# A register load tied behind a transposing transfer, and one k load traced five steps earlier, in an attention and expert kernel

## The chip, the cores and the metric

The kernel runs on one core of a Trainium2 chip. The metric is the device time of one execution in microseconds (us). Times below are either such a time or positions and durations in one execution that the hardware profiler recorded.

The engines are named as in the profile: PE (TensorE, with PEld for its weight loads), DVE (VectorE), ACT (ScalarE), POOL (GpSimd) and SP (SyncE), which here issues nearly all transfers. Each engine works through its own row of instructions in order, and an instruction that has to wait holds up all that stand behind it.

## The reference

Three blocks follow each other. The first is attention with random features for 4 batches of 8 heads, 576 tokens and 64 channels. `phi` projects q and k to 128 features and takes an exponential; each head then needs only `kv` and `z`, sums over the tokens.

```
q_p, k_p = (phi(q_s), phi(k_s))
kv = np.einsum('bhsm,bhsd->bhmd', k_p, v)
z = np.sum(k_p, axis=2)
num = np.einsum('bhsm,bhmd->bhsd', q_p, kv)
den = np.einsum('bhsm,bhm->bhs', q_p, z)[..., None] + 1e-06
return num / den
```

Its output, 2304 tokens of 512 channels, goes to a layer of 8 experts, in which every token belongs to the expert with the largest logit.

```
expert_idx = np.argmax(x @ w_gate, axis=1)
for e in range(E):
    xe = x[expert_idx == e]
    out[expert_idx == e] = gate_w * (np.maximum(xe @ w1[e], 0.0) @ w2[e])
```

The third block is a plain feed-forward layer, `h = x @ w_in`, `g = h / (1 + exp(-1.702 h))`, `g @ w_out`, with 2048 hidden channels.

## The kernel before

**Attention in quarters.** Each batch's 8 heads go in two halves of 4 heads, so there are 8 such pieces (the code's index `i`, called quarters here; `QB` is 2, the number of pieces of one batch). For each piece `kgen` makes the features of k and the sums `kv`, and `qgen` the features of q, the quotient (`num`, N in the code, L444) and its transposition for the experts (`tx`, `small`, L464 to L473). Ahead of that a piece has to be loaded and turned: `load_qk` (L253, L258) loads it to `m`, and `halves_T` splits it into two half-precision parts `hl` (ACT makes the first, POOL or DVE the second, L307 and L308), turns them with a transposing transfer on SP, `xT<-hl` (L309), and asks for the sums of squares. The projection `pr` (L350, L351) reads `xT`. `qgen` is a list of steps such as P0, X0, N0, each of which yields. In step number `KPRE` = 6 of piece `i` it loads k's piece `i + 2` and calls `halves_T` for it.

**Routing and experts.** After the second piece of a batch, `route_steps` computes the logits, counts the tokens of each expert (`ct_ps`, L561) and takes the expert with the most, `es` (L571). The expert's number comes into a register of SP by `values_load` (L604, a TENSOR_LOAD), and by that register `stage` loads the weights of that expert in 8 chunks of 512 KB, the first in two parts, from `w1` and `w2` (L674, `st<-in_moe_w_dram`). `rr` holds each token's expert and gate, and is stored by L609 and L612. `split_w` splits each chunk into a rounded part `wh` (ACT, L698) and the rest `wl` (POOL, the first chunk DVE, L700), and an expert matmul consists of three products of such parts (`mm3`, L136, `m_ps`).

**What sets the order.** The code is traced in one thread in which attention and experts take turns. A scheduler then places every instruction in the row of its engine by a simulated timeline of its own, so code that is traced in another place can move instructions on all engines. Loads, stores and transposing transfers share SP's row. A transfer is issued when the row comes to it and its inputs are there. Under `tc.high_priority()` stand the weight loads of the first batch. `tc.add_manual_dep` with the class NoSync says to the scheduler that one instruction comes after another on the same engine; no semaphore is waited on for it.

Of the kernel before, what the change touches and what calls it, by code (L numbers as in the profile page):

```python
# [22 lines left out]
def kernel(  # L23
# [13 lines left out]
    nc = tc.nc  # L37
# [24 lines left out]
    XQ = nc.sync  # L62
    DVE_LO = 1
    KPRE = 6
# [117 lines left out]
    NJ = 9  # L182
    QB = H // QH
    NQ = B * QB
    asked = []
    clock = [0]
    late = []

# [77 lines left out]
    def square_sum(m, c, sq, folds):  # L266
        nc.gpsimd.tensor_tensor(out=m[:, c], in0=m[:, c], in1=m[:, c], op=ALU.mult)
        w = D
        for _ in range(folds):
            w //= 2  # L270
            o = sq[:, c].unsqueeze(2) if w == 1 else m[:, c, 0:w]
            nc.gpsimd.tensor_tensor(out=o, in0=m[:, c, 0:w], in1=m[:, c, w:2 * w], op=ALU.add)
        if w > 1:
            nc.vector.tensor_reduce(out=sq[:, c], in_=m[:, c, 0:w], axis=AX.X, op=ALU.add)
        nc.scalar.activation(out=sq[:, c], in_=sq[:, c], func=ACTF.Copy, scale=sq_scale)

    def turned(src, i):
        m = src[i]
        xT = att.tile([P, NJ, P], F32, tag="xT", name="xT", bufs=3)
        sq = att.tile([P, NB], F32, tag="sq", name="sq", bufs=3)  # L280
        mv = m.rearrange("p (j two) d -> p j (two d)", two=2)
        for j in range(3):
            n = T if j < 2 else 1
            tp = pp.tile([P, T, P], F32, tag="m", name="tp", bufs=2)
            for x in range(n):
                nc.tensor.transpose(tp[:, x], mv[:, j * T + x], ident)
            c = slice(j * T, j * T + n)
            if FEV[j] == "a":
                nc.scalar.activation(out=xT[:, c], in_=tp[:, 0:n], func=ACTF.Copy)
            else:  # L290
                nc.vector.tensor_copy(xT[:, c], tp[:, 0:n])
        for c in (slice(0, 8), slice(8, NB)):
            square_sum(m, c, sq, FOLD)
        src[i] = (xT, sq, True)

    def halves_T(src, i, eng):
        sides[0] += 1
        if sides[0] <= FPX:
            return turned(src, i)
        if sides[0] - 1 in LO_DVE:  # L300
            eng = nc.vector
        m = src[i]
        hl = att.tile([P, NB, 2, D], F16, tag="hl", name="hl", bufs=2)
        xT = att.tile([P, NB, P], F16, tag="xT", name="xT", bufs=3)
        sq = att.tile([P, NB], F32, tag="sq", name="sq", bufs=3)
        for c in (slice(0, 8), slice(8, NB)) if i < FINE else (slice(0, NB),):
            nc.scalar.activation(out=hl[:, c, 0], in_=m[:, c], func=ACTF.Copy)  # L307
            eng.tensor_tensor(out=hl[:, c, 1], in0=m[:, c], in1=hl[:, c, 0], op=ALU.subtract)  # L308
            XQ.dma_start_transpose(out=xT[:, c], in_=hl[:, c].rearrange("p n a d -> p (n a d)"))  # L309
            square_sum(m, c, sq, FOLD_LATE)  # L310
        src[i] = (xT, sq, False)

# [15 lines left out]
    turn = {"N": 0, "X": 0, "A": 0}  # L328
# [85 lines left out]
    def qgen(i):  # L414
        b, qd = divmod(i, H // QH)
# [64 lines left out]
        for n, op in enumerate(Q_ORDER.split()):  # L480
            g = int(op[1])
            if op == "R0" and qd == 0:
                while x_done[0] < b - 1:
                    yield None
                xh_t[b] = (moe if b % 2 else xep).tile([P, KD, S], F32R, tag="xh", name="xh", bufs=1)
                xl_t[b] = (moe if b % 2 else xep).tile([P, KD, S], F32R, tag="xl", name="xl", bufs=1)
            if op[0] == "P":
                c = ph_P(i, src, qp, "qp", 3, g)
            else:
                c = {"X": X, "N": N, "R": XT}[op[0]](g)  # L490
            if n == 0 and i + 1 < NQ:
                load_v(i + 1)
            if n == KPRE and i + 2 < NQ:
                load_qk(k, k_in, i + 2, asked[-1] if i == QB + 1 else None)
                halves_T(k_in, i + 2, nc.vector if i + 2 < DVE_LO else nc.gpsimd)
            yield c
# [23 lines left out]
    def route_steps(b):  # L520
# [3 lines left out]
        for hf, tg in ((0, "n"), (1, "u")):  # L524
            c = slice(hf * HS, (hf + 1) * HS)
# [9 lines left out]
        for t in range(T + 1):  # L535
            n = P if t < T else TAIL
# [18 lines left out]
            out=ex, in0=lg, in1=rm.to_broadcast([P, T + 1, E]), op=ALU.subtract  # L555
# [6 lines left out]
            out=ct_ps.rearrange("p t e -> p (t e)"), lhsT=ones, rhs=oh.rearrange("p t e -> p (t e)")  # L562
# [13 lines left out]
        if b == B - 1:  # L576
            dg = att.tile([P, T * P + TAIL], F32, tag="dg", name="dg", bufs=1)
            for t in range(T + 1):
                n = P if t < T else TAIL
                nc.scalar.activation(  # L580
                    out=dg[:n, t * P:t * P + n], in_=ident[:n, :n], func=ACTF.Copy, scale=gate[:n, t, :]
# [5 lines left out]
        for t in range(T + 1):  # L587
# [9 lines left out]
            out=rr[:, :, 0:1], in0=eq, scalar=-float(2 * E), in1=ixf, op0=ALU.mult, op1=ALU.add  # L597
# [3 lines left out]
        nc.vector.tensor_tensor(out=total, in0=total, in1=hit, op=ALU.subtract)  # L601
        nc.vector.tensor_copy(rr[:, :, 1:2], gate)
        yield 0.5
        reg_t[b] = nc.values_load(  # L604
            es[0:1, 0:1], engines=[mybir.EngineType.SP], min_val=0, max_val=E - 1,
            skip_runtime_bounds_check_because="an index of the largest of E counts",
        )
        pump()
        nc.sync.dma_start(  # L609
            out=r_dram[b * S:b * S + T * P].rearrange("(p t) c -> p t c", t=T), in_=rr[:, 0:T]  # L610
# [70 lines left out]
    def pump(n=0):  # L681
        ahead = 2 * NW - 1 if prep["split"] < 2 else NST
        while prep["staged"] < min(max(prep["split"] + ahead, 2 * NW - 1), 2 * NW * B) and prep["staged"] // (2 * NW) in reg_t:
            stage(*divmod(prep["staged"], 2 * NW))
            prep["staged"] += 1
        while n and prep["split"] < min(prep["free"], prep["staged"]):
            split_w(*divmod(prep["split"], 2 * NW))
            prep["split"] += 1
            n -= 1
# [310 lines left out]
    if True:  # L1000
# [26 lines left out]
        while a_live:  # L1027
            if force == "a" or (force is None and done_a - lead <= A_RATIO * done_m):
                c = next(A, "end")
# [5 lines left out]
            else:  # L1035
                c = next(Mg)
# [363 lines left out]
        p = hp.tile([P, SETW], F32R, tag="y2", name="p2", bufs=1)  # L1400
# [29 lines left out]
    with tc.If(more > 0), tc.tile_pool(name="gp", bufs=1) as gp:  # L1430
        with tc.For_i(0, NT // P, 1) as w:
# [7 lines left out]
            xT = gp.tile([P, KD, P], F32, name="xT")  # L1439
# [13 lines left out]
            with tc.For_i(0, E, 1) as e:  # L1453
# [6 lines left out]
                with tc.If(cnt > 0):  # L1460
# [3 lines left out]
                    for f in range(NF1):  # L1464
                        wa = gp.tile([P, KD, P], F32, name="wa", bufs=2)
                        nc.sync.dma_start(
                            out=wa,
                            in_=w1[bass.ds(e, 1), :, f * P:(f + 1) * P].rearrange(
                                "o (k p) f -> p (o k) f", p=P
                            ),  # L1470
                        )
                        ps = pp.tile([P, P], F32, tag="m", name="g_ps", bufs=2)
                        for kk in range(KD):
                            nc.tensor.matmul(
                                out=ps, lhsT=wa[:, kk], rhs=xT[:, kk], start=(kk == 0), stop=(kk == KD - 1)
# [4 lines left out]
                    for dt in range(KD):  # L1480
                        wb = gp.tile([P, NF1, P], F32, name="wb", bufs=2)
                        nc.sync.dma_start(
                            out=wb,
                            in_=w2[bass.ds(e, 1), :, dt * P:(dt + 1) * P].rearrange(
                                "o (k p) d -> p (o k) d", p=P
                            ),
                        )
                        ps = pp.tile([P, P], F32, tag="m", name="g_ps", bufs=2)
                        for f in range(NF1):
                            nc.tensor.matmul(  # L1490
                                out=ps, lhsT=wb[:, f], rhs=ha[:, f], start=(f == 0), stop=(f == NF1 - 1)
# [53 lines left out]
```

## Time and profile before

| what | us |
|---|---|
| runs, not profiled | 764.91, 766.84, 766.99 |
| median of them | 766.84 |
| profiled execution | 766.79 |
| its span in the trace | 764.9 |

The span runs from the first recorded instruction to the last one; the device time contains 1.9 us beside it. The profile has busy time by engine, waits by what ended them, a timeline by engine, and windows, in which for any stretch the busy time of each engine, the granted clock of TensorE (1.00 is full speed) and the share of the DMA engines stand. The wait of an instruction is the idle time of its engine just before it, and `<-` in it names what came last.

### The profile page before, as it was taken

The page shows a single profiled execution, that of the slowest core. Times are in us where ns is not written, and L with a number is a line of the kernel's source. Part 1 is how long each engine was busy: PE and PEld are TensorE (multiplying, and loading weights), DVE is VectorE, ACT ScalarE, POOL GpSimd, SP SyncE. Part 2 cuts the span into 40 slices and gives each one's busy share as a digit, 9 for nine tenths or more (in the row PEclk, how much of TensorE's full clock was granted, in tenths as well). Part 3 has the DMA queues.
Part 4 walks back from the last instruction along what each step waited for, and adds up shares of the span by engine and source line. Part 5 has one row for each costly group of instructions (what it writes and reads, how often), then busy time and mean ns, then how long its engine had stood idle before and what let it go on. Part 6 is the DMA issues. An engine that isn't in the chain of part 4 may idle for free.

```text
span 764.9 us, 14360 instructions
## 1 busy us (share of the span) xinstructions
PE 737.1 (96%) x5559; PEld 715.1 (93%) x5559; DVE 527.5 (69%) x1188; ACT 337.5 (44%) x638; POOL 131.8 (17%) x78
## 2 busy tenths in 40 slices
PE   7998799998999999999999999999999999999997
PEld 6877789998999999998999999999999999999996
DVE  5866848583958577655879559981368777777774
ACT  5554554334623423332427565454576443444331
POOL 3563467604900522000000000000000000000000
PEclk9999799999999999999999999999999999999999
DMA  5447495539723544558155548972978544443311
GB/s 156 116 134 187 160 234 110 136 83 250 189 71 98 169 164 141 175 172 274 59 165 197 178 167 299 320 259 101 330 276 297 171 138 138 138 126 121 114 30 31
DMA packets 136715, 127.57 MB, mean 167 GB/s; under 512 B 58176, under 2 KB 120896, under 8 KB 135744
## 3 DMA queue, kind: packets, MB, share of 16 engines
q1 hardware_dynamic: 123936, 98.85, 44.6%
q10 hardware_dynamic: 12704, 27.73, 10.5%
q8 instruction: 45, 0.74, 0.4%
q14 instruction: 30, 0.25, 0.1%
HBM read 79.68 MB, written 40.40 MB: 157 GB/s over the span
## 4 chain that ended last, share of the span: by engine, by line
PE 80%; DMA 7%; DVE 5%; POOL 3%; ACT 2%; issue 2%; SPq 1%; ACTq 0%; POOLq 0%; DVEq 0%
PE m_ps L136 17%; PE qa L1249 13%; PE qa L1146 13%; PE qm L1249 7%; PE w_ps L136 5%; DMA st<-in_moe_w_dram 4%; PE pb L1249 3%; PE qm L1146 3%; PE qu L1146 3%; PE num L444 2%; POOL wl L700 2%; PE kv_ps L402 2%; PE qn L1146 2%; PE qt L1146 2%; DMA m<-in_k_dram 1%
## 5 line engine op out<-in xcount | busy, mean ns | idle before, releaser
L1146 PE MATMUL qa<-y,wi 128*128 128x384 f32 x576 | 109.2, 337 | 0.4 <-DVE g L901 0.4
L1146 PEld LDWEIGHTS qa<-y,wi 128*128 128x128 f32 x576 | 101.4, 188 | 0.8 <-DVE g L901 0.8
L136 PE MATMUL m_ps<-xh,wh 128*128 128x288 f32 x256 | 77.8, 304 | 0.7 <-DVE h1l L735 0.7
L136 PE MATMUL m_ps<-xh,wl 128*128 128x288 f32 x256 | 76.0, 298 | 0.0
L136 PE MATMUL m_ps<-xl,wh 128*128 128x288 f32 x256 | 75.8, 296 | 0.0
L700 POOL TENSOR_TENSOR wl<-st,wh 128x1024 fp32r<-128x1024 f32 x23 | 55.1, 2403 | 108.2 <-ACT wh L698 108.2
L359 DVE TENSOR_REDUCE small<-pr 128x4 f32<-128x512 f32 (+1 forms) x80 | 51.0, 638 | 16.1 <-PE pr L351 12.3
L698 ACT ACTIVATE wh<-st 128x1024 fp32r<-128x1024 f32 (+1 forms) x33 | 34.0, 1033 | 44.0 <-DMA st<-in_moe_w_dram 32.7
L735 DVE SCALAR_TENSOR_TENSOR h1l<-m_ps,h1h 128x288 fp32r<-128x288 f32 x64 | 28.9, 454 | 34.0 <-ACT h1h L732 34.0
L732 ACT ACTIVATE h1h<-m_ps 128x288 fp32r<-128x288 f32 x64 | 25.8, 405 | 55.3 <-PE m_ps L136 53.9
L136 PEld LDWEIGHTS m_ps<-xh,wh 128*128 128x128 f32 x256 | 48.1, 188 | 1.7 <-DVE h1l L735 1.4
L136 PE MATMUL m_ps<-h1h,wh 128*128 128x288 f32 x160 | 49.2, 307 | 0.0
L136 PEld LDWEIGHTS m_ps<-xl,wh 128*128 128x128 f32 x256 | 48.1, 188 | 0.1
L136 PEld LDWEIGHTS m_ps<-xh,wl 128*128 128x128 f32 x256 | 48.0, 188 | 0.2
L136 PE MATMUL m_ps<-h1h,wl 128*128 128x288 f32 x160 | 47.7, 298 | 0.3 <-POOL wl L700 0.3
L136 PE MATMUL m_ps<-h1l,wh 128*128 128x288 f32 x160 | 47.6, 297 | 0.0
L1249 PE MATMUL qa<-p,p 128*128 128x256 f32 x360 | 46.1, 282 | 1.1 <-DVE p L855 0.8
L1249 PE MATMUL qa<-p,gs 128*128 128x256 f32 x360 | 45.9, 282 | 0.0
L1249 PEld LDWEIGHTS qa<-p,p 128*128 128x128 f32 x360 | 44.1, 189 | 1.6 <-DVE p L855 1.0
L1249 PEld LDWEIGHTS qa<-p,gs 128*128 128x128 f32 x360 | 44.2, 189 | 0.0
L432 ACT ACTIVATE qpT<-tq 128x512 f32<-128x512 f32 (+1 forms) x40 | 22.1, 552 | 43.3 <-PE tq L430 38.6
L444 PE MATMUL num<-kv,qpT 128*128 128x65 f32 (+1 forms) x320 | 39.4, 267 | 0.7 <-ACT qpT L432 0.6
(213 smaller groups left out, 1835.1 us busy)
## 6 DMA issues: line engine op xcount, KB each, us to landing
g_dram<-g ACTq DMA_DIRECT2D x48, 384.0 KB, 3.9
st<-in_moe_w_dram SPq DMA_DIRECT2D x31, 512.0 KB, 5.0
pg<-g_dram SPq DMA_DIRECT2D x10, 1024.0 KB, 5.5
raw<-in_moe_w_in_dram SPq DMA_DIRECT2D x16, 512.0 KB, 3.8
gt<-g_dram SPq DMA_DIRECT2D x8, 1024.0 KB, 5.4
p<-wo_dram SPq DMA_DIRECT2D x6, 1024.0 KB, 7.3
yt<-y_dram SPq DMA_DIRECT2D x12, 384.0 KB, 5.4
vm<-in_v_dram SPq DMA_DIRECT2D x32, 128.0 KB, 3.2
```

The lines of the kernel that those rows point to most:

```text
L136: ins = nc.tensor.matmul(out=ps, lhsT=a, rhs=b, start=start and n == 0, stop=stop and n == 2)
L359: nc.vector.tensor_reduce(out=pm, in_=ps[:, :w], axis=AX.X, op=ALU.max, negate=on_act)
L402: nc.tensor.matmul(out=kv_ps[:, h, :], lhsT=kp[j // 2][:, j % 2, h2, :], rhs=vm[:, h, t, :], start=(t == 0), stop=False,)
L432: nc.scalar.activation(out=qt[i][:, :w], in_=tq[:, :w], func=ACTF.Exp)
L444: nc.tensor.matmul(out=ps[:n, c, h2, :], lhsT=lhsT, rhs=kv[:, h, :])
L698: nc.scalar.activation(out=hi[:, :, s], in_=st[:, :, s], func=ACTF.Copy)
L700: eng.tensor_tensor(out=lo[:, :, s], in0=st[:, :, s], in1=f32(hi)[:, :, s], op=ALU.subtract)
L732: nc.scalar.activation(out=hh[:, f], in_=ps, func=ACTF.Relu)
L735: nc.vector.scalar_tensor_tensor(out=hl[:, f], in0=ps, scalar=0.0, in1=f32(hh[:, f]), op0=ALU.max, op1=ALU.subtract)
L1146: ins = nc.tensor.matmul(out=ps, lhsT=w[:, a, ks], rhs=y[:, b, kk], start=start and kk + m == 0, stop=kk == 1 and m == 2, skip_group_check ...
L1249: ins = nc.tensor.matmul(out=ps, lhsT=x[:, f], rhs=w[i][:, f], start=start and f + m == 0, stop=f == NP - 1 and m == 2, skip_group_check=True,
```

## The change

Two edits, both on the place of instructions.

- In `qgen` of piece `QB` = 2 alone, the load of k's piece 4 and `halves_T` for it are traced at the first step instead of in step 6. `halves_T` remembers the last transposing transfer that it issued, in `turned_last`.
- In `route_steps` of the first batch, the instructions of `values_load` get an order-only dependence on that remembered transfer.

```diff
-    asked = []
+    asked, turned_last = [], [None]
...
-            XQ.dma_start_transpose(out=xT[:, c], in_=hl[:, c].rearrange("p n a d -> p (n a d)"))
+            turned_last[0] = XQ.dma_start_transpose(out=xT[:, c], in_=hl[:, c].rearrange("p n a d -> p (n a d)"))
...
-            if n == KPRE and i + 2 < NQ:
+            if n == (0 if i == QB else KPRE) and i + 2 < NQ:
...
+        seen = len(nc.cur_bb.bb.instructions)
         reg_t[b] = nc.values_load(
...
+        if b == 0:
+            for x in nc.cur_bb.bb.instructions[seen:]:
+                tc.add_manual_dep(
+                    x, turned_last[0].ins.name,
+                    mybir.DependencyInfo(mybir.DependencyClass.NoSync, mybir.DependencyReason.DATA),
+                    reason="behind the turn",
+                )
```

The lines behind the first edit keep their numbers until L604, which is L605 after it; the lines behind the second edit are 8 higher (L609 is L617, L674 is L682, L698 is L706).

The rows of SP around the first routing, before. `es` is the expert's number, `st` a weight chunk's landing place, `xT_1159` is k's piece 4 turned.

```order
L604 TENSOR_LOAD es_986
L674 ISA
L674 DMA st_1020<-in_moe_w1_dram 128x4x128
...
L674 DMA st_1033<-in_moe_w2_dram 128x2x512
L609 DMA r_dram_65<-rr_1011 128x8
L674 ISA
L674 DMA st_1254<-in_moe_w2_dram 128x2x512
L612 DMA r_dram_65<-rr_1011 64x2
L309 DMA_TRANSPOSE xT_1159<-hl_1158 128x18x128
L504 DMA x_dram_63<-xn_875 64x256
L309 DMA_TRANSPOSE xT_1458<-hl_1457 128x18x128
L253 DMA m_1613<-in_k_dram 128x4x256
```

The same stretch of SP in the changed kernel; `xT_902` is the same piece of k, under another number.

```order
L617 DMA r_dram_65<-rr_1025 128x8
L620 DMA r_dram_65<-rr_1025 64x2
L309 DMA_TRANSPOSE xT_902<-hl_901 128x18x128
L605 TENSOR_LOAD es_1000
L682 ISA
L682 DMA st_1034<-in_moe_w1_dram 128x4x128
...
L682 DMA st_1047<-in_moe_w2_dram 128x2x512
L504 DMA x_dram_63<-xn_875 64x256
L309 DMA_TRANSPOSE xT_1458<-hl_1457 128x18x128
L682 ISA
L682 DMA st_1254<-in_moe_w2_dram 128x2x512
```

Both stores of `rr` and the transposing transfer have moved ahead of the register load and of all weight loads. The ninth of these now stands behind the second transposing transfer.

The rows of PE at the same place, before, where the first expert matmuls begin (`wh0` and `wl0` are the first chunk's parts).

```order
L351 MATMUL pr_1236<-wl2_118,xT_710 128x128
L136 MATMUL m_ps_1071<-xh_546,wh0_1039 128x288
L136 MATMUL m_ps_1071<-xl_547,wh0_1039 128x288
L444 MATMUL num_1186<-kv_859,qpT_1109 128x65 x4
L136 MATMUL m_ps_1124<-xh_546,wh0_1039 128x288
L136 MATMUL m_ps_1124<-xl_547,wh0_1039 128x288
L136 MATMUL m_ps_1071<-xh_546,wl0_1040 128x288
```

And in the changed kernel, from the same `pr_1236` on.

```order
L351 MATMUL pr_1236<-wl2_118,xT_710 128x128
L444 MATMUL num_1186<-kv_859,qpT_1123 128x65 x4
L350 LDWEIGHTS xT_710
L350 MATMUL pr_1319<-wh2_117,xT_710 128x128
...
L351 MATMUL pr_1319<-wl2_118,xT_710 128x128
L444 MATMUL num_1275<-kv_859,qpT_1183 64x65 x4
L430 MATMUL tq_1284<-ident_79,qp_1234 128x128 x4
L350 LDWEIGHTS xT_866
L350 MATMUL pr_1468<-wh2_117,xT_866 128x128
```

Attention work of the pieces under way (two groups of `num`, two of `pr`, one of `tq`) has moved ahead of the first expert matmul.

The rows of ACT around the second routing, before; `wh2` is the third weight chunk of the second expert, `qpT` a turned feature of q.

```order
L432 ACTIVATE qpT_2265<-tq_2260 128x512
L386 ACTIVATE kp_2295<-kp_2295 128x512
L386 ACTIVATE kp_2371<-kp_2371 128x512
L275 ACTIVATE sq_2496<-sq_2496 128x18
L698 ACTIVATE wh2_2241<-st_2162 128x1024
L432 ACTIVATE qpT_2331<-tq_2326 128x512
L698 ACTIVATE wh3_2299<-st_2239 128x1024
L469 ACTIVATE xh_2375<-tx_2377 128x512
```

The same stretch of ACT in the changed kernel.

```order
L432 ACTIVATE qpT_2265<-tq_2260 128x512
L386 ACTIVATE kp_2295<-kp_2295 128x512
L386 ACTIVATE kp_2371<-kp_2371 128x512
L432 ACTIVATE qpT_2331<-tq_2326 128x512
L706 ACTIVATE wh2_2241<-st_2162 128x1024
L275 ACTIVATE sq_2496<-sq_2496 128x18
L706 ACTIVATE wh3_2299<-st_2239 128x1024
L469 ACTIVATE xh_2375<-tx_2377 128x512
```

`qpT_2331` has moved ahead of `wh2`. On SP, at that place, the load of k's piece of the same time (`m_2651`, 512 KB) has moved from behind the fourth chunk's load to ahead of the third one's, `st_2162`.

## Rows read from the trace of the kernel before

**Rows 1.** The page's first part: busy time, share of span and instructions, by engine.

```profile
PE 737.1 (96%) x5559; PEld 715.1 (93%) x5559; DVE 527.5 (69%) x1188; ACT 337.5 (44%) x638; POOL 131.8 (17%) x78
```

**Rows 2.** PE's waits, 50 to 130 us: waiting line, releaser, total us, times, longest.

```profile
PE pr L350 <- DMA xT<-hl: 1.9, 1, 1.9
...
PE m_ps L136 <- POOL wl L700: 0.3, 1, 0.3
```

**Rows 3.** SP's timeline: start us, duration us, line, operation, tiles, count.

```profile
90.10 0.88 SPq L609 DMA_DIRECT2D r_dram<-rr  x1
...
91.66 0.53 SPq L612 DMA_DIRECT2D r_dram<-rr  x1
92.92 6.89 SPq L309 DMA_TRANSPOSE xT<-hl  x1
```

**Rows 4.** L309 at 57 to 62, then landing at 92 to 101 (ns min/median/max).

```profile
L309 SPq DMA_TRANSPOSE xT<-hl x2: 1841/2212/2583, 57.6 to 61.3; - x2
...
DMA to landing us min/median/max: 4.0/4.3/4.6
...
DMA to landing us min/median/max: 9.0/11.3/13.7
```

**Rows 5.** L604 and the first eight weight loads, L674 (ns; starts; landing us).

```profile
L604 SPq TENSOR_LOAD <-es x1: 472/472/472, 84.3 to 84.3; - x1
...
L674 SPq DMA_DIRECT2D st<-in_moe_w_dram x8: 372/390/792, 85.0 to 89.2; - x8
...
DMA to landing us min/median/max: 2.8/6.6/9.2
```

**Rows 6.** DVE's timeline at the first routing.

```profile
85.47 0.17 DVE L596 SCALAR_TENSOR_TENSOR rr<-eq,ixf 128x5 f32<-128x5 f32 x1
...
88.44 0.69 DVE L700 TENSOR_TENSOR wl<-st,wh 128x512 fp32r<-128x512 f32 x1 [0.88 <-ACT wh L698]
...
92.41 0.68 DVE L380 TENSOR_TENSOR qp<-pr,mx 128x512 f32<-128x512 f32 x1
```

**Rows 7.** PE's timeline where the first expert matmuls begin.

```profile
88.62 0.38 PE L136 MATMUL m_ps<-xh,wh 128*128 128x288 f32 x1
...
88.97 1.00 PE L444 MATMUL num<-kv,qpT 128*128 128x65 f32 x8
89.78 0.38 PE L136 MATMUL m_ps<-xh,wh 128*128 128x288 f32 x1
...
92.76 0.23 PE L350 MATMUL pr<-wh,xT 128*128 128x128 f16 x1
...
95.05 0.40 PE L136 MATMUL m_ps<-xh,wh 128*128 128x288 f32 x1
```

**Rows 8.** ACT's first rounding of weights, and POOL's longest pause (idle before, in brackets).

```profile
87.77 0.63 ACT L698 ACTIVATE wh<-st 128x512 fp32r<-128x512 f32 x1 [0.54 <-DMA st<-in_moe_w_dram]
...
114.30 2.39 POOL L308 TENSOR_TENSOR hl<-m,hl 128x1152 f16<-128x1152 f32 x1 [5.11 <-DMA m<-in_q_dram]
```

**Rows 9.** ACT, PE and DVE around the second routing, from their timelines.

```profile
179.69 1.06 ACT L698 ACTIVATE wh<-st 128x1024 fp32r<-128x1024 f32 x1 [4.79 <-DMA st<-in_moe_w_dram]
...
181.28 0.44 PE L464 MATMUL tx<-ident,xn 128*128 128x128 f32 x2 [2.18 <-ACT qpT L432]
...
187.39 0.27 PE L466 MATMUL small<-ident,xn 64*128 64x64 f32 x1
...
186.36 0.22 DVE L473 TENSOR_TENSOR xl<-small,xh 128x64 fp32r<-128x64 f32 x1
```

**Rows 10.** Windows: length, busy us of PE, PEld, DVE, ACT, POOL, granted clock, DMA.

```profile
48.00:50.00 2.00, 1.11 (x7) 0.71 (x7) 1.83 (x5) 0.67 (x2) 1.92 (x2) 1.00 0.53 118
50.00:52.00 2.00, 2.00 (x10) 1.91 (x11) 1.90 (x8) 2.00 (x5) 1.22 (x1) 0.65 0.06 13
78.00:88.00 10.00, 7.22 (x47) 6.89 (x48) 9.35 (x52) 2.87 (x10) 4.80 (x3) 0.50 0.18 55
104.00:108.00 4.00, 2.13 (x24) 1.90 (x24) 2.57 (x10) 1.58 (x3) 2.83 (x2) 1.00 1.16 162
```

## The prediction

> **What bounds the kernel now.** I read the page's head first: TensorE (PE) is busy for 737.1 us, 96% of the span [rows 1], so only some 28 us of idle time can be won at all, and an edit that adds and removes no work can act only through PE's waits. The second view is PE's waits by what ended them, in the stretch around the first routing. There stand the two waits that the change can reach: 1.9 us at the projection of L350, ended by the transfer `xT<-hl`, and 0.3 us at an expert matmul, ended by POOL's `wl` [rows 2].
>
> The third view is SyncE's (SP) issues in order of time. It shows why `xT<-hl` is late. SP issues eight weight loads from 85.0 to 89.2 [rows 5], two small stores of the routing with a ninth load between them, and only then, at 92.92, the transposing transfer, which holds SP for 6.89 us [rows 3]. The two transposing transfers of that stretch landed 9.0 to 13.7 us after their issue; two others, at 57.6 and 61.3, ahead of which no weights were under way, took 4.0 to 4.6 us and held SP for 1.84 to 2.58 us [rows 4]. So the transfer stands behind some 4 MB of weights, and PE pays 1.9 us for it.
>
> **The change part by part.** No operation is added or removed, and the arithmetic is untouched. What changes is order: on SP at the first routing (load of k and its transposing transfer traced early, the register load tied behind that transfer), and, as the scheduler lays the rest out anew, on PE, DVE, ACT and SP as far as some 300 us. What PE does up to 88.6 us and from some 300 us on stands in the same order as before. k's halves are made at the same place of POOL's row too, so tracing them earlier costs nothing there.
>
> *1. The transposing transfer goes ahead of the weights: −1.9 us.* The changed kernel has on SP: two stores of `rr`, transposing transfer, register load, eight weight loads. The stores wait for `rr`, whose last piece DVE writes until 85.47 + 0.17 = 85.64 [rows 6]. They hold SP for 0.88 and 0.53 us [rows 3], with the gaps between issues until about 87.2. The transfer then finds no weights under way, so I take the short form of [rows 4]: it holds SP for 1.84 to 2.58 us and lands 4.0 to 4.6 us after its issue, at 91.2 to 91.8, against 92.92 + 13.7 = 106.6 before. PE asks for it no earlier than 106.6 − 1.9 = 104.7, so the whole wait goes.
>
> *2. The first weights come later: +1.9 us.* The register load holds SP for 0.47 us [rows 5], so the first weight load is issued at 87.2 + 2.2 + 0.47 and the gaps, about 89.95, instead of 85.0: 5.0 us later. It landed 2.8 us after its issue [rows 5]; with 0.1 or 0.2 us more behind the transfer it lands at 92.9. ACT rounds it in 0.63 us [rows 8], so the first expert matmul can start at 93.65 instead of 88.62 [rows 7], again 5.0 us later. Behind that wait stands all of PE's work, since PE keeps its order. What covers it is the work that the new order puts ahead: one group of `num`, from 88.97 to the next matmul at 89.78, and the run of `pr`, `num`, `tq` and `pr` from 92.76 to 95.05 [rows 7], together 0.81 + 2.29 = 3.1 us. So 5.0 − 3.1 = 1.9 us of new idle time appear. They fall in two places: at `tq`, which needs `qp` from DVE, and at the first matmul on `wh0`. `qp` was written from 92.41 to 93.09, behind two `wl` of 0.69 us each [rows 6] that now come after it, so it is there at about 91.9; PE gets there at about 90.6 and has 1.1 us of work (`tq`, `pr`) after it. So even with earlier weights PE can't reach the expert before 93.0, which gives a lower bound of 93.0 − 88.62 − 3.1 = 1.3 us. The upper bound takes SP's longer hold (0.4 us) and half a microsecond more until the first landing: 2.8 us. I take 1.9, the value of the short forms.
>
> This is where a rule speaks against the edit. The Trainium skill, "DMA: Bandwidth & Descriptors", section "Rules for kernel authors", says that a transfer is to be issued early, with work done under it and its semaphore waited on late, so that its setup is overlapped. By it the weights, which PE uses as soon as they are there, wouldn't be held back for a transfer that is needed 13 us later; uncovered, term 2 would be 5.0 us and the time 769.1.
>
> *3. The later weights: −0.3 us.* With every weight 5 us later, ACT's rounding and POOL's residues come 5 us later as well. POOL had 5.11 us of idle time ahead of its work at 114.30 [rows 8], so the delay ends there, and the last residue, `wl7`, is finished about 1 us later than before. PE asks for it some 5 us later, because projections stand ahead of that group of matmuls in the new order. So the 0.3 us [rows 2] goes; if that cover failed, it would become up to 1 us.
>
> *4. The second routing: −0.5 us.* Around 181 us PE waited 2.18 us at `tx` for ACT's `qpT`, which stood behind the rounding at 179.69 of a weight chunk that had landed late [rows 9]. In the new order this `qpT` stands ahead of the rounding, so that wait goes. Not all of it is gained: the next transposition into `small`, at 187.39, needs the residue `xl` that ends at 186.36 + 0.22 = 186.58 [rows 9], and that hangs on the next chunk. It had 0.8 us of slack; PE arriving 2.2 us earlier waits 1.4 us there, and 0.8 is left. On the other side SP now issues a load of k (512 KB) ahead of that third chunk. Of the eight weight loads the first landed at 85.0 + 2.8 = 87.8 and the last at 89.2 + 9.2 = 98.4 [rows 5], some 1.5 us apart, so this can move the chunk by 0 to 1.5 us, and the earlier place of the routing in PE's order (six expert matmuls fewer ahead of it) takes a part back. I take 0.3 us of it: −0.8 + 0.3 = −0.5, with ends −2.2 (the wait simply goes) and −0.8 + 1.5 = +0.7 (the chunk is late by the whole load).
>
> **The sum.** −1.9 + 1.9 − 0.3 − 0.5 = −0.8 us. The profiled execution took 766.79 us, 1.9 us more than its span; the median of the three runs is 766.84, so both bases agree. 766.8 − 0.8 = 766.0 us. A measurement of this kernel can tell about 0.3%, or 2.3 us, from no change, so this is "the same". With the lower ends of terms 2 and 4 the sum is −1.9 + 1.3 − 0.3 − 2.2 = −3.1 (763.7), with the upper ends and term 3's +1.0 it is −1.9 + 2.8 + 1.0 + 0.7 = +2.6 (769.4).
>
> **The rivals.**
> *Late weights* (slower): the transposing transfer holds SP for 6.9 us, as at 92.92 [rows 3], and not for 2.2. The first weights then come another 4.7 us later, term 2 is 1.9 + 4.7 = 6.6, and the sum −1.9 + 6.6 − 0.3 − 0.5 = +3.9, or 770.7 us. Each microsecond of hold beyond 2.2 costs one, so it is slower by more than can be measured from a hold of 5.3 us on. For it: 6.07 and 6.89 us are the nearest holds in time. Against it: both followed the weights, and here nothing of that size goes ahead. The skill's rule above, with its 769.1, belongs to this case.
>
> *The clock falls* (slower): the new idle time lies close together between 90 and 94 us. Before, PE was busy for only 1.11 of the 2 us from 48 to 50, and the granted clock, 1.00 until then, was 0.65 in the mean of the next two; in 78 to 88 it stood at 0.50 throughout, which is the lower of its two levels, 1.2 GHz instead of 2.4 [rows 10]. The first of these is at least 0.35 × 2 / 0.5 = 1.4 us at half speed, and costs 0.7 us or more; 10 us at half speed cost 5. That gives 766.7 to 771.0. Against it: from 104 to 108 PE was busy for only 2.13 of 4 us and the clock stayed at 1.00 [rows 10], about as full as I expect the emptiest 4 us here (4 − 1.9). It decides once the waits between 90 and 94 come to more than those 1.9 us.
>
> *The waits simply go* (faster): the weights are there by 93.0 and the chunk at the second routing isn't late, nor the residue behind it: 763.7 us. For it: the order ahead of PE has room at both places. Against it: it needs both low ends at once.
>
> *The transfer isn't early after all* (the change doesn't do what it says): the new order shows it ahead of the register load, so only a late `rr` or a long hold could bring this about, and both delay the weights too, which is the first rival.
>
> **How the numbers follow.** Forecast as worked out, 763.9 to 768.5: 0.58. The waits simply go: 0.19. Late weights: 0.11. The clock falls: 0.12, about half of it beyond 0.3%. With the forecast's tails, faster by over 0.3% (under 764.5) gets 0.22, within 0.3% 0.58, slower (over 769.1) 0.20. The range leaves out the outer parts of both slow rivals and a little at the low end: 763.4 to 770.0.
>
> **What would show it right or wrong.** In the changed kernel PE's wait for `xT<-hl` at L350 is gone, the first weight load is issued near 90.0, the first expert matmul starts at 93 to 94, and some 1.9 us of idle time stand on PE between 90 and 94, ended by DVE's `qp` and ACT's `wh`, with a granted clock of 1.00. At the second routing the 2.2 us at `tx` are gone and 1 to 2 us stand at `small`. The forecast is wrong if the transposing transfer holds SP for more than 3 us, if the first weight lands after 94, if the clock falls once more, or if both places agree and the time differs: then something that I hold for unchanged has moved.

## The result, and the profile after

The changed kernel is slower. Its median is 769.98 us (15 runs, 767.19 to 775.55), that of the kernel before 766.84 us (15 runs in the same stretch, 761.51 to 769.53). The ratio is 1.0058, with a 95% interval of 1.0035 to 1.0081: about 4.4 us, where 0.8 us of gain had been forecast. (The ratios here are those on record, from runs taken beside each other; they are not the quotients of the medians, which here differ by 3.1 us.) The median lies inside the stated range of 763.4 to 770.0 us only by 0.02 us, and on the slow side, where a gain was forecast; that is luck. A second comparison, in the second set of experiments below, gave 1.0062 (1.0036 to 1.0087). The profiled execution took 769.56 us, with a span of 767.7 us. Single runs of either kernel spread over 8 us, so below three profiles of each kernel are used, not one.

The page's line of busy time answers to [rows 1]: the work is the same, 737.8 against 737.1 us of PE.

```profile
span 767.7 us, 14364 instructions
PE 737.8 (96%) x5559; PEld 715.7 (93%) x5559; DVE 528.0 (69%) x1188; ACT 338.0 (44%) x638; POOL 131.9 (17%) x78
```

PE's waits from 76 to 130 us answer to [rows 2] (columns as there). The waits for `xT` and for `wl` are gone, as forecast. Those for `h1l`, `wh` and `xn` are new, and the one for `qp` (0.5 us before) has become two of 0.6 us. `wh` and `qp` were forecast, `h1l` and `xn` were not.

```profile
PE m_ps L136 <- DVE h1l L743: 1.8, 1, 1.8
PE m_ps L136 <- ACT wh L706: 1.5, 1, 1.5
PE tq L430 <- DVE qp L380: 1.1, 2, 0.6
PE num L444 <- DVE xn L455: 0.6, 1, 0.6
```

On PE's timeline they stand at these places, which answer to [rows 7]. The counting matmul `ct_ps` (L561) stands ahead of everything that moved on PE and is the mark from which I count: it stood at 80.31 us before (first row) and stands at 77.37 here (second row).

```profile
80.31 0.62 PE L561 MATMUL ct_ps<-oh,ones 128*128 128x40 f32 x2 [4.12 <-DVE oh L552]
```

```profile
77.37 0.62 PE L561 MATMUL ct_ps<-oh,ones 128*128 128x40 f32 x2 [4.16 <-DVE oh L552]
...
88.22 0.65 PE L444 MATMUL num<-kv,qpT 128*64 128x65 f32 x8 [0.57 <-DVE xn L455]
89.48 0.63 PE L430 MATMUL tq<-ident,qp 128*128 128x128 f32 x4 [0.61 <-DVE qp L380]
92.08 0.40 PE L136 MATMUL m_ps<-xh,wh 128*128 128x288 f32 x1 [1.53 <-ACT wh L706]
...
117.27 0.40 PE L136 MATMUL m_ps<-h1h,wh 128*128 128x288 f32 x1 [1.82 <-DVE h1l L743]
```

The first expert matmul came 88.62 − 80.31 = 8.3 us behind that mark before, and comes 92.08 − 77.37 = 14.7 us behind it now: 6.4 us later, where I had said 5.0. SP's timeline, which answers to [rows 3], shows where the weights stood; the first row is that of the first weights before.

```profile
84.97 5.03 SPq L674 DMA_DIRECT2D st<-in_moe_w_dram  x8
```

```profile
82.72 0.36 SPq L617 DMA_DIRECT2D r_dram<-rr  x1
83.13 0.52 SPq L620 DMA_DIRECT2D r_dram<-rr  x1
84.73 2.08 SPq L309 DMA_TRANSPOSE xT<-hl  x1
88.12 4.94 SPq L682 DMA_DIRECT2D st<-in_moe_w_dram  x8
93.16 0.82 SPq L504 DMA_DIRECT2D x_dram<-xn  x1
94.08 9.25 SPq L309 DMA_TRANSPOSE xT<-hl  x1
```

The transposing transfer held SP for 2.08 us, as forecast. But between the second store's end at 83.65 and the transfer there is a pause, and between the transfer's end at 86.81 and the first weight at 88.12 another. The queue's own waits name the first (SP's waits, 70 to 100 us), and the row of L605 the second: the register load took 1.03 us here, against 0.47 in [rows 5].

```profile
SPq L309 <- PE pr L351: 1.0, 1, 1.0
...
L605 SPq TENSOR_LOAD <-es x1: 1032/1032/1032, 86.9 to 86.9; - x1
```

So the transfer waited for PE: its destination `xT` is one of a ring of three buffers, and the projections L350 and L351 of an older piece still read that buffer. The first weight was issued 88.12 − 77.37 = 10.75 us behind the mark, against 84.97 − 80.31 = 4.66 before.

### The profile page after: what moved, and what is told of

Same layout as the page of the kernel before. It is cut to its first block, busy times and chain, and to the rows that moved or that the text cites. A ratio compares the mean times of both kernels' runs of the same rounds, so it can differ in the third digit from the quotient of the medians.

```text
span 767.7 us, 14364 instructions
## 1 busy us (share of the span) xinstructions
PE 737.8 (96%) x5559; PEld 715.7 (93%) x5559; DVE 528.0 (69%) x1188; ACT 338.0 (44%) x638; POOL 131.9 (17%) x78
## 4 chain that ended last, share of the span: by engine, by line
PE 87%; DMA 4%; DVE 3%; SPq 1%; ACT 1%; issue 1%; POOL 1%; POOLq 0%; ACTq 0%
PE m_ps L136 21%; PE qa L1257 13%; PE qa L1154 13%; PE qm L1257 7%; PE w_ps L136 5%; PE num L444 3%; PE pb L1257 3%; PE qm L1154 3%; PE qu L1154 3%; PE kv_ps L402 2%; PE tq L430 2%; DMA m<-in_k_dram 2%; DMA st<-in_moe_w_dram 2%; PE qn L1154 2%; PE pr L344 2%; PE qt L1154 2%
## 5 line engine op out<-in xcount | busy, mean ns | idle before, releaser
L706 ACT ACTIVATE wh<-st 128x1024 fp32r<-128x1024 f32 (+1 forms) x33 | 34.1, 1035 | 41.8 <-DMA st<-in_moe_w_dram 26.2
```

Of the source, the lines that this page charges most:

```text
L706: nc.scalar.activation(out=hi[:, :, s], in_=st[:, :, s], func=ACTF.Copy)
```

## The experiments

Twelve runs in three sets; the runs of a set have the same runs of the kernel before beside them. Ratios are against it, with the 95% interval. "After" means the changed kernel.

### The two edits apart, and two ways to mend them

**The early trace alone** (no dependence of the register load). The dependence alone changes nothing: `turned_last` then holds a transfer that was issued long before, and all rows of all engines stand as before, so it was not run.

```diff
-        if b == 0:
-            for x in nc.cur_bb.bb.instructions[seen:]:
-                tc.add_manual_dep(
-                    x, turned_last[0].ins.name,
...
```

> The early trace of k's load and halves alone, no dependence of the register load. On SP the weights then stand first again, and the transposing transfer moves only ahead of the ninth weight load and the two small stores. My theory is that the loss comes from the weights standing behind the transposing transfer and from what then stands behind them, so it should be gone: PE's wait for xT between 0 and 1.9 us, no wait for wh at the first expert matmul, 764.5 to 767 us, ratio 0.997 to 1.000 against the kernel before. The rival that the early trace by itself shuffles the rows and costs the time gives about 770 us, ratio 1.004.

Measured: 767.22 us against 764.57, ratio 1.0035 (1.0007 to 1.0063). In its rows the weights stand first, and the transfer stands between the eighth and the ninth. PE's waits, 76 to 130 us:

```profile
PE m_ps L136 <- POOL wl L701: 2.1, 1, 2.1
PE m_ps L136 <- ACT wh L699: 1.1, 1, 1.1
PE m_ps L136 <- DVE h1l L736: 0.5, 1, 0.5
```

They fall at the later chunks (115.06 and 118.11 us), not at the first matmul. ACT's timeline shows the half `hl` of k's next piece waiting for its load (idle time in brackets), and the last chunk's `wh` behind it; `wl` follows on POOL, behind the other half.

```profile
112.11 1.16 ACT L307 ACTIVATE hl<-m 128x1152 f16<-128x1152 f32 x1 [2.89 <-DMA m<-in_k_dram]
...
113.95 1.06 ACT L699 ACTIVATE wh<-st 128x1024 fp32r<-128x1024 f32 x1
```

So the early trace alone brought no gain, though the wait for `xT` was down to 0.2 us in this execution. It lost about 2.7 us, where both edits together lose 4.4; the intervals overlap. My expectation fell, and the rival's 1.004 fits. Late weights are not what this kernel lost by: its first weight was issued 81.96 − 77.31 = 4.65 us behind the mark, as before. But both transposing transfers now held SP for 7.9 to 8.0 us, and k's next load behind them was issued 29.6 us behind the mark, against 23.3 to 26.4 in three profiles of the kernel before.

**ACT's half behind the two `h1h`.** In after, ACT came to the half `hl` of k's next piece ahead of two `h1h`, as ACT's timeline of after shows: a late gate row, then `hl` at 115.26, then `h1h`, then PE at 117.27. The half waited for k's load for 0.18 us only; most of the delay is the gate row's 2.89 us and the 1.16 us that the half itself takes.

```profile
112.64 1.21 ACT L638 ACTIVATE gb<-row 128x512 f32<-128x512 f32 x2 [2.89 <-DMA row<-gate_dram]
...
115.26 1.16 ACT L307 ACTIVATE hl<-m 128x1152 f16<-128x1152 f32 x1 [0.18 <-DMA m<-in_k_dram]
116.33 0.69 ACT L740 ACTIVATE h1h<-m_ps 128x288 fp32r<-128x288 f32 x2
```

```diff
-            nc.scalar.activation(out=hl[:, c, 0], in_=m[:, c], func=ACTF.Copy)
+            hi = nc.scalar.activation(out=hl[:, c, 0], in_=m[:, c], func=ACTF.Copy)
+            follow(hi, h1_last[0] if i == QB + 3 else None)
...
-                nc.scalar.activation(out=hh[:, f], in_=ps, func=ACTF.Relu)
+                h1_last[0] = nc.scalar.activation(out=hh[:, f], in_=ps, func=ACTF.Relu)
```

> The changed kernel with one more order-only dependence: ACT's half of k's piece 5 (hl at L307) stands behind the last two h1h of the first expert instead of ahead of them. Theory: the 1.8 us that PE waited for h1l at 117.3 us in the changed kernel came from ACT standing at that half, which waited for the late load of k; it goes, and about 1.8 us of the loss with it: some 768.2 us, ratio about 1.002. The rival that this wait only moves to the next thing that is late (the last weight residue, or ACT's next row) gives 769 to 770 us, ratio 1.003 to 1.005.

Measured: 771.68 us against 764.57, ratio 1.0105 (1.0072 to 1.0137). The wait for `h1l` was indeed gone from 76 to 130 us, so its cause is shown: `h1h` standing behind `hl` in ACT's row. The time didn't follow, and is above what both the theory and the rival gave, since this one dependence moved other rows too. At the second routing (130 to 215 us) PE now waited for:

```profile
PE tx L465 <- ACT qpT L433: 3.9, 1, 3.9
PE pr L351 <- DVE qp L381: 0.8, 1, 0.8
```

**The stores behind the register load**, so that nothing that waits for the routing stands ahead of the transfer. In the diff `s1` and `s2` are the two stores of `rr`, and `regs` the instructions of the register load.

```diff
+        if b == 0:
+            for s in (s1, s2):
+                for x in regs:
+                    tc.add_manual_dep(
+                        s.ins, x.name,
+                        mybir.DependencyInfo(mybir.DependencyClass.NoSync, mybir.DependencyReason.DATA),
+                        reason="behind the register",
+                    )
```

> The changed kernel with one more order-only dependence: the two stores of rr stand behind the register load. The transposing transfer then heads SP's row at this place, with nothing ahead that waits for the routing, and is issued as soon as its halves are there, about 10 us before the register load, instead of behind the stores. Theory: the weights are issued at the time of the kernel before (some 4.6 us after the counting matmul), the 1.5 us at wh and most of the 2.7 us of new waits around the first expert matmul go, and so does the wait for xT: 764.5 to 767 us, ratio 0.997 to 1.000, with the 1.8 us at h1l perhaps still there in part. The rival that the new order of PE and ACT costs the time, wherever the weights stand, gives 769 to 770 us.

Measured: 770.26 us against 764.57, ratio 1.0088 (1.0055 to 1.0122). My expectation fell, and the reason is one row of SP's waits from 66 to 100 us. The transfer now headed the row, and stood there for 14.5 us:

```profile
SPq L309 <- PE pr L351: 14.5, 1, 14.5
```

It was issued at 84.59, the first weight at 87.89, 10.7 us behind the mark (77.23): just as late as in after, where the transfer, too, went 84.73 − 77.37 = 7.4 us behind the mark (84.59 − 77.23 = 7.4 here). Not the stores held the transfer but the buffer, and what stands behind it, the register load, waits with it.

**Both dependences.**

> Both dependences: the stores of rr behind the register load, and ACT's half of k's piece 5 behind the two h1h. Theory: no wait for xT, none for wh, none for h1l between 88 and 130 us; 764 to 766 us, ratio 0.996 to 0.999. If what is left is decided by the second routing, it is equal to the kernel before, 766 to 768 us.

Measured: 768.98 us against 764.57, ratio 1.0064 (1.0040 to 1.0088). No wait for `h1l`, 0.9 us for `wh`, 3.9 us at the second routing. It is no better than after, and the expected 764 to 766 us didn't come.

### A buffer of its own, and the second routing

**After once more.**

> The changed kernel once more, beside the other three of this set, so that all have the same runs of the kernel before to be compared with, and for a second profile. Expected: ratio about 1.006, as it was; around the first routing again some 2.7 us at xn, qp and wh and 1.5 to 2 us at h1l. My theory for the second routing is that its waits now lie so that the clock falls there as a rule: then this profile too has a stretch of half speed between 180 and 200 us. The rival, that the fall in the first profile was chance, gives none there.

Measured: 769.75 us against 765.28, ratio 1.0062 (1.0036 to 1.0087). Its profile shows 1.7 us at `wh`, 0.6 at `h1l`, 1.1 at `qp`, 0.6 at `xn` again, and a mean granted clock of 0.94 from 170 to 200 us, as in the first, so the clock did fall there again. In the three profiles of the kernel before it was 1.00, 0.94 and 1.00. Over all runs, however, the mean granted clock was 0.989 for after (12 runs) and 0.988 for the kernel before (32 runs) in this set, so a lower clock is not shown to be the rule.

**After, with a buffer of its own.** k's piece 4 is turned into a tile of another pool that stands empty until about 250 us; for a fourth buffer in the ring there is no room.

```diff
-        xT = att.tile([P, NB, P], F16, tag="xT", name="xT", bufs=3)
+        if i == QB + 2 and src is k_in:
+            xT = wz.tile([P, 2 * NB // 2, P], F16, tag="a", name="xT", bufs=1)
+        else:
+            xT = att.tile([P, NB, P], F16, tag="xT", name="xT", bufs=3)
...
```

The lines left out make two other tiles of that pool (`z` and `raws`) only when `prep_outs`, the work that uses them, is begun, so that the place is free until then.

> The changed kernel with k's piece 4 turned into a buffer of its own (a tile of another pool that stands empty until about 250 us) in place of the ring of three. In the kernel with the stores moved behind, SP stood for 14.5 us at the transposing transfer until PE's last projection from the ring's oldest buffer was through, so the theory is that not the stores but this buffer holds the transfer, and with it all weights. With a buffer of its own the transfer goes some 12 us earlier, the register load follows at once when es is there, the wait for wh and xT both go: 0.995 to 1.000 against the kernel before. The rival (weights late for another reason, or the new order of PE costs the time) gives 1.004 to 1.009 as the others.

Measured: 763.50 us against 765.28, ratio 0.9981 (0.9956 to 1.0005). Its interval lies wholly below that of after. SP's timeline shows the transfer 11 us ahead of the weights, and these 81.39 − 76.36 = 5.0 us behind the mark:

```profile
70.64 2.31 SPq L312 DMA_TRANSPOSE xT<-hl  x1
...
81.39 5.81 SPq L685 DMA_DIRECT2D st<-in_moe_w_dram  x8
```

From 76 to 130 us no wait for `xT` or `wh` is left; the 0.8 us at `h1l`, 0.9 at `qp` and 0.9 at `pr` are.

**The kernel before with that buffer.**

> The kernel before with nothing but that buffer of its own. In its rows the transposing transfer then stands ahead of the register load without any dependence. Theory: the 1.9 us at xT go, no other wait comes in at the first expert; 0.995 to 0.999. If it equals the kernel with the change and the buffer, the two edits of the change add nothing of their own once the buffer is free; rival: it stays at 1.000 because the 1.9 us move to the next late thing (weights' residue, the gate's row).

Measured: 763.73 us against 765.28, ratio 1.0005 (0.9983 to 1.0028), so no change. Its rows are those of the run above on every engine but for one small row of ACT: with the buffer free the scheduler puts the transfer ahead by itself, and the two edits of the change add nothing. The two runs are in effect one kernel measured twice, 0.998 and 1.0005. The wait for `xT` is gone, but the rows ahead of the routing have changed too, and two waits at `pr` for ACT's `kp` came to 3.0 us. So it shows what held the weights, and not what the 1.9 us are worth alone.

**The second routing as it was.** After, with the load of k's piece 7 behind the fourth chunk of the second expert.

```diff
-load_qk(k, k_in, i + 2, asked[-1] if i == QB + 1 else None)
+load_qk(k, k_in, i + 2, asked[-1] if i == QB + 1 else fourth[-1] if i == 2 * QB + 1 else None)
...
+                if (b, c) == (1, 3):
+                    fourth.append(ins)
```

> The changed kernel with the load of k's piece 7 ordered behind the fourth weight chunk of the second expert, as it stood in the kernel before. It tells what the second routing costs: theory, 0.5 to 2.5 us of the loss (the chunk lands earlier, xl too, fewer waits there, and no fall of the clock), so a ratio of 1.002 to 1.005 where the changed kernel has 1.006. The rival, that the whole loss stands at the first routing, gives the ratio of the changed kernel.

Measured: 769.37 us against 765.28, ratio 1.0067 (1.0042 to 1.0091), which is that of after. The second routing had 1.5 us of waits. So the place of k's load there isn't what costs the time. The clock's fall at the second routing is not cleared by this run: its mean from 170 to 200 us was 0.94 here as well.

### How typical the first profiles were

**The kernel before, twice more**, the second time as a single execution.

> The kernel before, once more, as a measure of what no change at all gives in these comparisons (ratio 0.999 to 1.001), and for a second profile: my theory takes the 1.9 us at xT, the 0.3 us at wl and the 2.2 us at tx as the rule. If they are missing or much smaller in this execution, the first profile was not typical, and the gain that I expected from the first term was smaller from the start.

> A third profile of the kernel before. Theory: 1 to 2 us at xT, no wait at wh, about 2 us at tx. Rival: the wait at xT is missing here.

Measured: 764.58 us against 765.05, ratio 0.9991 (0.9966 to 1.0016); the single execution took 761.36 us. PE's waits of the first of them, 76 to 130 us, and then those of the second:

```profile
PE tq L430 <- DVE qp L380: 0.7, 1, 0.7
PE m_ps L136 <- ACT wh L698: 0.5, 1, 0.5
```

```profile
PE ct_ps L561 <- DVE oh L552: 4.8, 1, 4.8
PE m_ps L136 <- ACT wh L698: 1.0, 1, 1.0
PE tq L430 <- DVE qp L380: 0.5, 1, 0.5
```

In neither is there a wait for `xT` or `wl`. The transfer took the same place in SP's row, held SP as long, 6.86 and 6.83 us, and landed 11.1 and 10.7 us after its issue, not 13.7 [rows 4]. The row of L309 in each:

```profile
L309 SPq DMA_TRANSPOSE xT<-hl x1: 6862/6862/6862, 89.3 to 89.3; - x1
...
DMA to landing us min/median/max: 11.1/11.1/11.1
```

```profile
L309 SPq DMA_TRANSPOSE xT<-hl x1: 6835/6835/6835, 89.5 to 89.5; - x1
...
DMA to landing us min/median/max: 10.7/10.7/10.7
```

**After a third time**, as a single execution.

> A third profile of the changed kernel. Theory: 2.7 to 2.9 us of waits at xn, qp and wh around the first expert matmul again, 0.6 to 1.8 us at h1l, 2 to 3 us at the second routing; rival: these vary so much from one execution to the next that none of them is the rule.

Measured: 767.98 us. The same waits at the same places:

```profile
PE m_ps L136 <- ACT wh L706: 2.0, 1, 2.0
PE m_ps L136 <- DVE h1l L743: 1.1, 1, 1.1
PE tq L430 <- DVE qp L380: 1.1, 2, 0.6
PE num L444 <- DVE xn L455: 0.6, 1, 0.6
```

**The weights a little later.** The kernel before, with the register load behind the two stores alone, which are traced ahead of it for that.

```diff
+            for x in nc.cur_bb.bb.instructions[seen:]:
+                for s in (s1, s2):
+                    tc.add_manual_dep(
+                        x, s.ins.name,
+                        mybir.DependencyInfo(mybir.DependencyClass.NoSync, mybir.DependencyReason.DATA),
+                        reason="behind the stores",
+                    )
```

> The kernel before with the register load ordered behind the two stores of rr alone, so that the weights come some 2 to 3 us later and not 6, with the transposing transfer behind them as before. Theory (the loss grows with the weights' delay): PE's waits at the first expert matmul 0 to 1 us, 766 to 768 us where the kernel before has 765, ratio 1.001 to 1.004. The rival that any new order of these rows costs 4 to 5 us gives 1.005 or more; the rival that only the transposing transfer ahead of the weights costs gives 1.000.

Measured: 775.68 us against 765.05, ratio 1.0122 (1.0085 to 1.0158). The first weight was issued 86.73 − 79.44 = 7.3 us behind the mark, 2.6 us later than before, and yet it is the slowest of all. Its waits at `wh` and at the second routing (76 to 130 us, 130 to 215 us):

```profile
PE m_ps L136 <- ACT wh L707: 3.2, 2, 2.8
...
PE tx L464 <- ACT qpT L432: 4.1, 1, 4.1
```

Its mean granted clock was lower too, 0.984 against 0.989. So a loss that grows with the delay, as I had expected, isn't what the runs show. Nor is the transposing transfer ahead of the weights needed for a loss: here it stands behind them. The runs show that each of the six kernels in which the weights come later than before (7.3 to 10.8 us behind the mark) lost 0.6 to 1.2%, while the two with the weights at their old time (5.0 us) and the transfer out of their way, after and before with the buffer, lost nothing. The early trace alone, with the weights at their old time and the transfer right behind them, stands between: 0.35%. How large the loss is, depends on what else the new order moves: here the second routing alone had 4.1 us.

## Why the prediction was wrong

**The steps that failed.** The forecast was −0.8 us, the comparison shows about +4.4. PE's waits, in the mean of three profiles of after against three of the kernel before, show which terms went wrong (us, rounded).

| term | forecast | measured |
|---|---|---|
| 1, the wait for `xT` | −1.9 | −0.6 |
| 2, the waits for `xn`, `qp`, `wh` | +1.9 | +2.4 |
| 3, the waits for `wl` and `h1l` | −0.3 | +1.1 |
| 4, the second routing | −0.5 | −0.2 |
| sum | −0.8 | +2.6 |

So the terms that failed are 3, whose path was wrong, and 1, whose size was. The premise that the edit "can act only through PE's waits" failed as well; the paragraph on the sum has the rest.

**Term 1, the gain of 1.9 us.** The mechanism was right, the size was one execution's. The wait for `xT` stood in one of three profiles of the kernel before (1.9, 0, 0), because the transfer's landing varied from 10.7 to 13.7 us after its issue and PE asked for it in between, at 11.9 to 12.4 us. The mean gain was nearer to 0.6 us. Term 3's 0.3 us at `wl` was there in the first profile only as well.

**Term 2, the cost of the later weights.** Forecast 1.9 us (1.3 to 2.8); the three profiles of after show 0.6 + 0.6 + 1.5 = 2.7, 0.6 + 0.6 + 1.7 = 2.9 and 0.6 + 0.6 + 2.0 = 3.2 us at `xn`, `qp` and `wh`. The kernel before had 0, 0.5 and 1.0 us at `wh` itself, so the new part is 2.4 us in the mean, within the range. Two pieces of it were wrong all the same. I let the transfer go as soon as SP was free. It also needs a free destination, and the ring of three gives one only when PE has read the oldest piece, as the 14.5 us in the run with the stores behind show; the description of the kernel before, by which a transfer is issued when its inputs are there, lacks that. In after this wait was 1.0 us. Beside that the register load took 1.03 us, not 0.47. Together the first weight was issued 10.75 us behind the mark instead of 4.66, 6.1 us later and not 5.0. That the transfer finds no weights under way was right: it held SP for 2.08 us and landed 4.9 us after its issue. The wait for `qp` came as forecast; that for `xn` I hadn't seen.

**Term 3, the later weights.** I followed the delay along POOL, where the pause did swallow it, and not along ACT's row. There `h1h` stood behind the half `hl` of k's next piece: 1.8, 0.6 and 1.1 us of waits for `h1l`, and none in the run with the half behind the `h1h`.

**Term 4, the second routing.** Forecast −0.5 us. All waits from 130 to 215 us came to 2.5, 2.5 and 2.4 us before and 2.9, 2.1 and 1.7 after, −0.2 in the mean, and putting k's load back changed nothing. This term was about right.

**The sum.** From 76 to 130 us, without the wait at the counting matmul, PE's waits came to 2.7, 1.2 and 1.5 us before and 5.0, 4.0 and 4.8 after: 2.8 us more in the mean. With −0.2 from the second routing that is 2.6 of the measured 4.4 us. Windows from the mark to the first matmul of the third block (`qu`) show where the rest can be; this is the first profile of before, and then of after (columns as in [rows 10]).

```profile
80.31:399.43 319.12, 312.10 (x2592) 301.00 (x2593) 219.26 (x652) 122.27 (x238) 92.46 (x43) 0.99 0.58 158
```

```profile
77.37:402.14 324.77, 314.66 (x2592) 303.22 (x2593) 219.16 (x652) 122.87 (x238) 92.55 (x43) 0.98 0.55 155
```

The stretch took 319.1, 322.2 and 317.2 us in the three profiles of before and 324.8, 323.9 and 323.0 in those of after, 4.3 us more in the mean; the mark stood at 77.5 and 77.6 us in the mean, and what follows the stretch took 365.2 to 365.5 us in all six. So the whole loss stands in this stretch. PE was idle in it for 7.0, 7.0 and 6.1 us before and for 10.1, 8.3 and 8.0 after, which is 2.1 more. The other 2.2 us are busy time: the same 2592 matmuls took 312.1, 315.2 and 311.1 us before and 314.7, 315.5 and 314.9 after, at a granted clock of 0.99, 0.98 and 0.99 before and 0.98 in all three of after. In these six executions that closes the account. Whether the clock's half is the rule stays open. The profiled executions of before had a mean clock of 0.990, 0.990 and 0.995, above the mean of its runs; over all runs it was 0.987 (15 runs) and 0.989 (12) for after, and 0.988 (32) and 0.989 (17) for before, and 0.001 of it is about 0.8 us of 765 (an estimate).

Open, too, is how the loss divides between the late weights and k's next load, since the runs don't part them. That load was issued 23.3 to 26.4 us behind the mark in the three profiles of before and 21.2 us with the buffer, but 28.1 to 28.5 in after, 29.6 with the early trace alone and 36.1 in the slowest kernel. Against it as the only cause: 26.9 us in the run with the half behind the two `h1h`, which lost 1.05%.

**The rivals.** None came true as written. Late weights had the right side and 770.7 us, but its condition, a hold of 6.9 us, didn't come: the transfer held SP for 2.08 us, and the first weight was 6.1 us later than before, not 5.0 + 4.7 = 9.7. That its time is near the measured one is luck; I had given it 0.11. The clock did fall, in part: behind the waits at the first expert matmul in two of the three profiles of after, and at the second routing in all three. In the first of them it stayed at 1.00 from 92 to 98 us; in the second it went down there, with PE busy for 1.74 of the 4 us ahead.

```profile
88.00:92.00 4.00, 1.74 (x22) 1.45 (x19) 2.18 (x8) 1.14 (x3) 0.00 (x0) 1.00 0.61 160
92.00:94.00 2.00, 2.00 (x10) 1.81 (x10) 2.00 (x5) 2.00 (x7) 0.00 (x0) 0.51 1.06 365
```

The last rival said that only a late `rr` or a long hold could keep the transfer from being early; a buffer that is still read is a third way, and the one that came. The Trainium skill, "DMA: Bandwidth & Descriptors", section "Rules for kernel authors", has a transfer issued early and waited on late. For the weights the runs agree with it: the six kernels with later weights took 1.0058 to 1.0122 times as long as the kernel before.

## What to carry to other kernels

Before a transfer is put ahead of others in a queue, ask for everything that it waits for: its input, and also who still reads the buffer that it writes, since all that stands behind it in the queue waits for that reader too. A wait of 1 or 2 us that ends with a transfer's landing should be seen in more than one profile before it is counted as a gain. And where something is delayed, follow it along the row of every engine that handles it, since what harms is the work that stands behind it there.

## What the runs showed of the hardware

The register load of the first routing took 0.47 us where SP had issued nothing for 7 to 11 us (three profiles of before, the early trace alone, both kernels with the buffer), and 0.96 to 1.07 us right behind a transposing transfer that was still under way (three profiles of after and four of its variants). A transposing transfer isn't needed for that: right behind the two stores of `rr` it took 0.72 us, and at the fourth routing, 0.6 us behind a store of `y`, 1.01 to 1.29 us. The issue of the transposing transfers around the first routing held SP for about 2 us with no weights ahead of them (2.08 in after, 2.31 with the buffer) and for 6.8 to 9.3 us behind the weights (6.89 before, 9.25 in after), once for 5.64 us (both dependences). The same transfer at the same place in the row landed 10.7, 11.1 and 13.7 us after its issue in three executions.
